# A seven-product down projection in four steps of the first token block, with the second block's residual rows parked in device memory

## The chip, the cores and the metric

The kernel runs on one core of one Trainium2 chip. The metric is the device time of one execution in microseconds (us), the median of a few executions. TensorE multiplies matrices, VectorE and ScalarE read its results from PSUM, GpSimd works on SBUF, and SyncE issues the DMAs. The profile calls them PE (PEld for its weight loads), DVE, ACT, POOL and SP. In a program each engine executes its own instructions strictly in the order in which they were written.

## What is computed

The input x is 2048 tokens by 640 features in float32. Two sublayers with a residual each:

```python
h  = x + irfft2(rfft2(layernorm(x)) * (w_r + 1j * w_i))     # spectral filter over tokens and features
z  = layernorm(h)
h2 = h + ((z @ w_gate) * (z @ w_up)) @ w_down               # bilinear GLU, 640 -> 1728 -> 640
```

The change touches the second sublayer alone, and what of the first one's output waits for it.

## The kernel before, in words

**Number format.** Every matrix operand of the GLU is held as two float32r parts, a high and a low one. A product of two operands is three matmuls: high by high, high by low, low by high. "Splitting" a tile means that ACT writes the high part and DVE or POOL the low part.

**Tiles and blocks.** The 2048 tokens are 16 tiles of 128 rows. The first sublayer ends with one addition per tile into the residual rows `X[t]` (`acc`, L505). Tiles 0 to 7 are token block 0 and lie in the SBUF buffer `XH[0]` (tag `xh0`); tiles 8 to 15 are block 1 and lie in `XH[1]` (tag `xh1`). Each is 128 by 8 x 641 float32. All through block 0 of the GLU the rows of block 1 lie idle in `xh1`: they are only read, for the mean and variance and at the end to be normalised.

**Steps.** For each block the 1728 hidden features are 14 chunks, taken in seven steps of two chunks: step `p` holds chunks 2p and 2p+1, and the order is 6, 0, 1, 2, 3, 4, 5 (L1009). Step 6 is computed plainly. In the others `strassen` (L929) makes gate and up of one chunk for the block's 1024 tokens, as two halves of 512, with 54 matmuls of 512 columns; its products go to three PSUM banks called `p11`, `acc_a` and `p53`. ACT copies `acc_a` to `p1` (L960), later to `u2` (L973) and `p53` to `m5` (L979); DVE adds `p11` into `p1` (L970). The hidden tiles that come out are kept split in numbered units of `ht` (`unit`, L723); unit 6 lies in the buffer `ex`.

**The down projection of a step runs inside the next step.** There are two forms.

- Plain (`down`, L747): for each of the 8 token tiles of the block 12 matmuls of 320 columns (10 for step 6), then one DVE addition into `X[t]` (L508). The 8 tiles are called between the products of the next step's first chunk (`some`, L933), and after each one entry of the list `fill` is executed (L937): block 0 uses that list for the 32 small operations that take mean and variance of block 1's rows (L132 to L161).
- Seven-product (`mixed_down`, L884): the 2 by 2 block product with seven block products in place of eight, 84 matmuls in place of 96, in 16 pieces that are woven one by one behind the matmul triples of the next step's first chunk (`tick`, L943). It takes other hidden operands (`mixed_first` and `mixed_second`, which form sums and differences on DVE), other weight operands (`load_mixed`, L849, sums on POOL), and room for them: `EX[0]`, 128 by 8 x 641, which holds half of the weight operands (`wo`) and unit 6, called `ex` in the profile. What DVE and ACT still owe of the hidden units when a woven chunk begins is the list `pending`; `flush(1)` executes one entry after each woven piece.

Before the change steps 0 to 4 of **block 1** are seven-product. `EX[0]` is then the buffer of block 0's rows, which are finished and written out (L1090). Block 0 has plain steps only, since both row buffers are in use.

**The passage from block 0 to block 1.** In chunk 11 of block 0 SP loads the plain weights of chunks 13 and 12 (`load_direct`, one DMA to `draw`, two to `raw`), ACT takes their high parts (`wdir`, L463, by side[1], right after the `p1` addition), and ACT normalises the eight tiles of block 1 (L525, by side[2]). Then eight plain downs of step 5 alternate with the transposes of the normalised tiles (L1045 to L1058), and 90 matmuls against `wdir` follow.

**Weights.** `load_raw` brings 640 KB of chunk weights to `stage` (called `raw`); `prep` turns them into split operands with ACT and POOL. All DMAs named here are issued by SP, in the order in which the program names them, and SP does not go past one whose wait is not over.

Of the kernel before, what the change touches and what calls it, by code (L numbers as in the profile page):

```python
# [46 lines left out]
def tile_spectral_glu(ctx: ExitStack, tc: tile.TileContext, x, wf, wgu, wlast, wdown, wdlast,  # L47
# [43 lines left out]
    XH = [keep.tile([P, 8 * (D + 1)], F32, tag=f"xh{h}", name=f"x{h}") for h in range(2)]  # L91
    XP = [XH[t // 8][:, t % 8 * (D + 1):(t % 8 + 1) * (D + 1)] for t in range(NT)]
    X = [xp[:, 0:D] for xp in XP]
    cct = keep.tile([P, P], F32, name="cct")
    ident = keep.tile([P, P], F32, name="ident")

# [408 lines left out]
    def acc(t, ps, total=None):  # L505
        xv = X[t].rearrange("p (a b) -> p a b", a=2)
        if total is None:
            tt(xv, ps[:, :, 0:320], xv, op=OP.add)  # L508
        else:
            nc.vector.scalar_tensor_tensor(xv, ps[:, :, 0:320], 1.0, xv, op0=OP.mult, op1=OP.add, accum_out=total)  # L510
# [152 lines left out]
    for t in range(NT):  # L663
        for k in tside[t]:
            turn_mm(k)
        if t + 2 < NT:
            unfold(t + 2, dside[t], tside[t])
        else:
            for k in tside[t]:
                turn_hi(k)  # L670
                turn_lo(k)
        if t + 3 < NT:
            id_mm(t + 3)
        for f in aside[t]:
            f()
        if t == NT - 3:
            ht = home("qm", [P, 8192], "ht", F32R)
            hts, t3 = cut(ht, 0, 3, 2, 2, 512), cut(ht, 6144, 2, 2, 512)
            banks("a", "pglu")
            gu(NC - 1, 0)  # L680
        is1_mm(t)
        acc(t, PY[t], total[:, t:t + 1] if t < 8 else None)
        if t == NT - 2:
            late = gate_parts(NC - 1, 0, 0)
    transp(6)
# [35 lines left out]
        return copies, sums, high, low  # L721

    def unit(u):  # L723
        v = ht[:, 1024 * u:1024 * u + 1024] if u < 6 else EX[0][:, (3840, 1920)[u - 6]:][:, 0:1024]
        return v[:, 0:512], v[:, 512:1024]

    def high_of(u, src):
        act(unit(u)[0], src, AF.Copy)  # L728
# [56 lines left out]
    def flush(n=8):  # L785
        for h in pending[:n]:
            h()
        del pending[:n]
# [140 lines left out]
    def strassen(c, blk, h, ahead, downs, side, fine=()):  # L929
# [3 lines left out]
        def some(n):  # L933
            for _ in range(n):
                if downs:
                    downs.pop(0)()
                    pop(1)  # L937

        def at(n):
            for f in side.get(n, ()):  # L940
                f()

# [22 lines left out]
        if ahead and not woven:  # L965
# [1 line left out]
            flush(2)  # L967
            ahead[1]()
            flush()
        tt(p1, p11, p1, op=OP.add)  # L970
        at(1)
        product(acc_a, ws, 0, t2, start=False)
        act(u2, acc_a, AF.Copy)  # L973
        flush()
        if ahead and woven:
            ahead[0]()
            ahead[1]()
# [35 lines left out]
    for n, (blk, p) in enumerate(steps):  # L1013
        if p == 6:
# [28 lines left out]
            else:  # L1043
                copies, sums, high, low = prep(0, blk)
                js = [4, 5, 6, 7, 0, 1, 2, 3]  # L1045
                for j in range(8):
                    transp(8 + j)
                    if j >= 1:
                        down(*prev, js[j - 1], True)
                    if j % 4 == 3:  # L1050
                        fifth(range(5 + j, 9 + j))
                    if j == 3:
                        copies()
                        sums()
                    if j == 5:
                        high()
                        low()
                down(*prev, js[7], True)  # L1058
                gu(NC - 1, 0)
                gate_parts(NC - 1, 0, s13)()  # L1060
# [24 lines left out]
                fs, cs = scale_shift(range(8, 16), None)  # L1085
                fill.extend(fs + cs)
            continue
        mixed = blk == 1 and p < 5
        if mixed and p == 0:
            EX[0] = home("xh0", [P, 8 * (D + 1)], "ex", F32R)  # L1090
        wdn = load_mixed(p) if mixed else load_d(p)
        downs, fine = [], []
        if prev[2] is None:
# [3 lines left out]
        if mixed:  # L1097
            units, hs = None, (mixed_first(), mixed_second())
        else:
            units = [(2 * k, 2 * k + 1) for k in (count % 3, (count + 1) % 3)] if blk == 0 else [(2, 7), (1, 0)]  # L1100
            hs = [plain_h(u[1], u[0]) for u in units]
        for ci in range(2):
            c = 2 * p + ci
            side = {}
            ahead = None
            if c == 0:
                side[0] = [*t34(1), lambda j=first_wd: issue(j)]
            if c < 11:
                ahead = prep(c + 1, blk)
                side[5] = [lambda c=c: load_raw(c + 2)] if c < 10 else []  # L1110
            if ci == 0 and mixed:
                side[2] = [wdn[0], wdn[1]]
                side[6] = [wdn[2]]
            elif ci == 0:
                side[3] = [lambda wdn=wdn: issue(wdn)]
            if c == 11 and blk == 0:
                pop(len(fill))
                dj = load_direct(1, [wk([P, D], "draw"), stage[:, 0:640], stage[:, 640:1280]])
                side[1] = [lambda: issue(dj[0]), lambda: issue(dj[1]), lambda: load_raw(0)]

                def low(ks):
                    for k in ks:
                        if k == 0:
                            TJ["z"] = home("qr", [P, 6, D], "zt")
                        normalise(8 + k, TJ["z"][:, k] if k < 6 else wk([P, D], "z"))

                side[2] = [lambda: low(range(8))]
            strassen(c, blk, hs[ci], ahead, downs if ci == 0 else [], side, fine if ci == 0 else ())
            count += 1
        prev = (blk, p, units)  # L1130
# [134 lines left out]
```

## Time and profile before

| | |
|---|---|
| median of 3 runs | 721.1 us (720.89 to 722.38) |
| the profiled execution | 720.87 us |
| its span, first to last instruction | 719.1 us |
| mean granted TensorE clock | 1.000 |
| PE busy | 694.4 us, 97% |
| DVE, ACT, POOL busy | 445.0, 294.0, 333.8 us |

The profile below is of that one execution. A row of the timeline gives the start in us from the span's start, the busy time, the engine, the line of the kernel, the operation, the tiles (out<-in) and, in brackets, how long the engine stood idle before it and what ended that. A row of the windows gives for one stretch its length, then for each engine the busy time and the number of instructions (counting those that reach into it), then the clock column, the DMA share and the GB/s. In the rows, the matmuls of `strassen` write `e` and have 512 columns, those of the down projection write `y` and have 320.

### The profile page before, as it was taken

Reading aid. Unit: us, or ns where it says so; the run is one execution under the profiler, and the core shown is the slowest. Engines: PE = TensorE matmul, PEld = TensorE weight load, DVE = VectorE, ACT = ScalarE, POOL = GpSimd, SP = SyncE. Lnnn points to the kernel's source line nnn. Section 1 sums busy time; section 2 is a strip of 40 time slices with the busy share of each in tenths; the row PEclk is TensorE's granted clock in tenths of the full one; section 3 lists DMA queues with packets and bytes.
Section 4 is the critical chain, followed back from the end, with each engine's and each line's share of the span. In section 5 each row is a group of like instructions: output and inputs, shape, how many; then the busy total and the mean of one; then the engine's idle time right before and its main releaser. Section 6 shows DMA issues by size and latency. Waiting matters only on the chain.

```text
span 719.1 us, 10059 instructions
## 1 busy us (share of the span) xinstructions
PE 694.4 (97%) x3832; PEld 611.6 (85%) x3832; DVE 445.0 (62%) x787; ACT 294.0 (41%) x554; POOL 333.8 (46%) x310
## 2 busy tenths in 40 slices
PE   7899998999999999999999998999999999999998
PEld 7788997977878898989898988789888888888887
DVE  7968887797965453636334436565666666565654
ACT  4756666355543223223323245352334243424320
POOL 3300114332154554546454543138696877767610
PEclk9999999999999999999999999999999999999999
DMA  9405765000221212110011222221110203030203
GB/s 337 170 1 165 229 212 188 1 1 0 74 75 37 73 37 74 37 55 25 36 71 36 93 74 80 90 88 38 63 47 24 88 0 111 1 106 4 74 0 147
DMA packets 20927, 55.04 MB, mean 77 GB/s; under 512 B 2320, under 2 KB 6928, under 8 KB 20880
## 3 DMA queue, kind: packets, MB, share of 16 engines
q1 hardware_dynamic: 20304, 52.70, 21.3%
q0 software_dynamic: 288, 1.48, 0.6%
q8 instruction: 30, 0.49, 0.3%
q10 hardware_dynamic: 288, 0.23, 0.1%
q14 instruction: 17, 0.14, 0.1%
HBM read 49.16 MB, written 5.24 MB: 76 GB/s over the span
## 4 chain that ended last, share of the span: by engine, by line
PE 78%; DVE 13%; issue 4%; ACT 3%; POOL 1%; DMA 1%; DVEq 0%; POOLq 0%; ACTq 0%
PE e L82 42%; PE y L82 24%; PE re L82 2%; PE im L82 2%; PE u L341 2%; PE eo L82 2%; DVE fold L191 1%; DVE x L906 1%; DVE fold L196 1%; PE im L391 1%; PE im L390 1%; PE ir L382 1%; ACT zt L525 1%; DVE x L510 1%; DVE bits L215 1%
## 5 line engine op out<-in xcount | busy, mean ns | idle before, releaser
L82 PE MATMUL e<-xt,wst 128*128 128x512 f32 x864 | 214.6, 391 | 1.2 <-DVE ht L656 1.1
L82 PEld LDWEIGHTS e<-xt,wst 128*128 128x128 f32 x864 | 159.1, 188 | 30.9 <-DVE ht L656 1.6
L82 PE MATMUL y<-wd,ht 128*128 128x320 f32 x1048 | 171.3, 310 | 4.3 <-DVE x L508 3.1
L82 PEld LDWEIGHTS y<-wd,ht 128*128 128x128 f32 x1048 | 160.8, 188 | 13.3 <-DVE x L508 3.6
L703 POOL TENSOR_TENSOR wst<-raw,wst 128x1024 fp32r<-128x1024 f32 x24 | 57.9, 2412 | 113.2 <-ACT wst L702 108.0
L508 DVE TENSOR_TENSOR x<-y,x 128x640 f32<-128x640 f32 x79 | 65.0, 823 | 71.7 <-PE y L82 71.5
L728 ACT ACTIVATE ht<-e 128x512 fp32r<-128x512 f32 x47 | 27.5, 596 | 126.5 <-DVE e L797 101.0
L719 POOL TENSOR_TENSOR wst<-raw,wst 128x896 fp32r<-128x896 f32 (+1 forms) x46 | 65.1, 1438 | 21.4 <-ACT wst L714 21.4
L82 PE MATMUL e<-t,wst 128*128 128x512 f32 x288 | 71.9, 390 | 0.0
L906 DVE TENSOR_TENSOR x<-y,x 128x640 f32<-128x640 f32 x60 | 49.3, 823 | 28.4 <-PE y L82 28.0
L82 PEld LDWEIGHTS e<-t,wst 128*128 128x128 f32 x288 | 53.3, 188 | 9.7
L464 POOL TENSOR_TENSOR wd<-draw,wd 128x640 fp32r<-128x640 f32 x18 | 28.8, 1624 | 66.8 <-ACT wd L463 66.8
L986 DVE TENSOR_TENSOR m<-e,m 128x512 f32<-128x512 f32 x24 | 16.5, 689 | 52.1 <-PE e L82 51.6
L732 DVE TENSOR_TENSOR ht<-e,ht 128x512 fp32r<-128x512 f32 x47 | 32.2, 685 | 19.1 <-ACT ht L728 18.8
L82 PE MATMUL e<-xt,wdir 128*128 128x512 f32 x180 | 41.9, 392 | 1.1 <-DVE q L494 1.1
L82 PEld LDWEIGHTS e<-xt,wdir 128*128 128x128 f32 x180 | 33.5, 188 | 8.3 <-ACT xt L547 1.3
L702 ACT ACTIVATE wst<-raw 128x1024 fp32r<-128x1024 f32 x24 | 25.4, 1056 | 35.2 <-DMA raw<-in_wgu_dram 35.2
L714 ACT ACTIVATE wst<-raw 128x896 fp32r<-128x896 f32 (+1 forms) x48 | 30.0, 676 | 19.4 <-POOL raw L708 18.7
L82 PE MATMUL e<-ht,wst 128*128 128x512 f32 x144 | 37.7, 391 | 0.0
L207 PE MATMUL im<-bits,fold 128*128 128x128 f32 x192 | 30.0, 292 | 6.6 <-DVE fold L196 2.3
L409 POOL CAST qr<-bits 1x128 fp32r<-1x128 f32 x16 | 4.5, 280 | 68.0 <-DVE qr L406 68.0
L207 PEld LDWEIGHTS im<-bits,fold 128*128 128x128 f32 x192 | 24.6, 193 | 11.2 <-DVE fold L196 5.6
(210 smaller groups left out, 1165.0 us busy)
## 6 DMA issues: line engine op xcount, KB each, us to landing
raw<-in_wgu_dram SPq DMA_DIRECT2D x24, 640.0 KB, 3.9
wts<-in_wf_dram SPq DMA_DIRECT2D x16, 644.0 KB, 4.1
draw<-in_wdown_dram SPq DMA_DIRECT2D x24, 320.0 KB, 4.5
x<-in_x_dram SPq DMA_DIRECT2D x16, 320.5 KB, 6.0
out_dram<-x SPq DMA_DIRECT2D x15, 320.0 KB, 2.2
bits<-in_mm_dram SPq DMA_DIRECT2D x32, 128.0 KB, 3.9
raw<-in_wgu_dram SPq DMA_DIRECT2D x4, 320.0 KB, 3.8
draw<-in_wdlast_dram SPq DMA_DIRECT2D x4, 320.0 KB, 2.9
```

Of the source, the lines that this page charges most:

```text
L82: nc.tensor.matmul(o, l, r, start=start, stop=stop, skip_group_check=True)
L207: nc.tensor.matmul(pm[:, k * P:(k + 1) * P], l, c, start=n == 0, stop=n == len(ls) - 1)
L464: los.append(lambda r=r, a=a, b=b: engine.tensor_tensor(w[:, 1, a:b], r, f32(w[:, 0, a:b]), op=OP.subtract))
L508: tt(xv, ps[:, :, 0:320], xv, op=OP.add)
L702: act(wa[:, 0], stage[:, 0:1024], AF.Copy)
L703: nc.gpsimd.tensor_tensor(wa[:, 1], stage[:, 0:1024], f32(wa[:, 0]), op=OP.subtract)
L714: act(ws[:, 0, o:o + b - a], stage[:, a:b], AF.Copy)
L719: ptt(ws[:, 1, o:o + b - a], stage[:, a:b], f32(ws[:, 0, o:o + b - a]), op=OP.subtract)
L728: act(unit(u)[0], src, AF.Copy)
L732: engine.tensor_tensor(lo, src, f32(hi), op=OP.subtract)
L906: tt(xv, PQ[q][:, :, 0:320], xv, op=OP.add)
L986: tt(m5, acc_a, m5, op=OP.add)
```

## The change

Steps 1 to 4 of block 0 take the seven-product form too. To make room, the residual rows of block 1 go to device memory while block 0 runs its GLU.

- **Spill.** After the first sublayer's last addition to each of tiles 8 to 15, SP writes the tile to a DRAM tile `spill` (8 DMAs of 320 KB).
- **Room.** In block 0, `EX[0]` is the buffer `xh1`, taken at step 1. By then the mean and variance of block 1's rows have to be done, so the list `fill` is emptied in step 0: two entries behind each plain down instead of one, and five at each of the fixed places (`at`) of chunk 1.
- **Bring back.** `bring_back`, called ahead of chunk 11 of block 0, takes `xh1` again and has SP load the 8 tiles. It stands in the program ahead of `load_direct`. Normalising is spread over three places of chunk 11: four tiles at side[3], two at side[6], two at side[5].
- **The `p1` addition** stands behind the second product and the `flush` where the chunk is woven, in both blocks.
- **Units.** Step 5 keeps its hidden tiles in units 4, 2, 1, 0 in both blocks; the former unit 7 in `EX[0]` is gone.
- **Passage.** Among the eight last downs of block 0 the transposes of the fifth slices (`fifth`) come ahead of the down of the same turn, and the `high` and `low` splitting of chunk 0's weights comes after the loop.

```diff
@@ -91,6 +91,8 @@
     XH = [keep.tile([P, 8 * (D + 1)], F32, tag=f"xh{h}", name=f"x{h}") for h in range(2)]
     XP = [XH[t // 8][:, t % 8 * (D + 1):(t % 8 + 1) * (D + 1)] for t in range(NT)]
     X = [xp[:, 0:D] for xp in XP]
+    kept = ctx.enter_context(tc.tile_pool(name="kept", bufs=1, space=bass.MemoryType.DRAM))
+    spill = [kept.tile([P, D], F32, tag=f"sp{i}", name=f"sp{i}") for i in range(8)]
     cct = keep.tile([P, P], F32, name="cct")
     ident = keep.tile([P, P], F32, name="ident")
 
@@ -680,6 +682,8 @@
             gu(NC - 1, 0)
         is1_mm(t)
         acc(t, PY[t], total[:, t:t + 1] if t < 8 else None)
+        if t >= 8:
+            nc.sync.dma_start(spill[t - 8], X[t])
         if t == NT - 2:
             late = gate_parts(NC - 1, 0, 0)
     transp(6)
@@ -721,8 +725,15 @@
         return copies, sums, high, low
 
     def unit(u):
-        v = ht[:, 1024 * u:1024 * u + 1024] if u < 6 else EX[0][:, (3840, 1920)[u - 6]:][:, 0:1024]
+        v = ht[:, 1024 * u:1024 * u + 1024] if u < 6 else EX[0][:, 3840:4864]
         return v[:, 0:512], v[:, 512:1024]
+
+    def bring_back():
+        XH[1] = home("xh1", [P, 8 * (D + 1)], "xb")
+        for t in range(8, NT):
+            o = (t - 8) * (D + 1)
+            X[t] = XH[1][:, o:o + D]
+            nc.sync.dma_start(X[t], spill[t - 8])
 
     def high_of(u, src):
         act(unit(u)[0], src, AF.Copy)
@@ -934,9 +945,11 @@
             for _ in range(n):
                 if downs:
                     downs.pop(0)()
-                    pop(1)
+                    pop(2)
 
         def at(n):
+            if c == 1 and blk == 0:
+                pop(5)
             for f in side.get(n, ()):
                 f()
 
@@ -967,11 +980,14 @@
             flush(2)
             ahead[1]()
             flush()
-        tt(p1, p11, p1, op=OP.add)
+        if not woven:
+            tt(p1, p11, p1, op=OP.add)
         at(1)
         product(acc_a, ws, 0, t2, start=False)
         act(u2, acc_a, AF.Copy)
         flush()
+        if woven:
+            tt(p1, p11, p1, op=OP.add)
         if ahead and woven:
             ahead[0]()
             ahead[1]()
@@ -1045,16 +1061,15 @@
                 js = [4, 5, 6, 7, 0, 1, 2, 3]
                 for j in range(8):
                     transp(8 + j)
+                    if j % 4 == 3:
+                        fifth(range(5 + j, 9 + j))
                     if j >= 1:
                         down(*prev, js[j - 1], True)
-                    if j % 4 == 3:
-                        fifth(range(5 + j, 9 + j))
                     if j == 3:
                         copies()
                         sums()
-                    if j == 5:
-                        high()
-                        low()
+                high()
+                low()
                 down(*prev, js[7], True)
                 gu(NC - 1, 0)
                 gate_parts(NC - 1, 0, s13)()
@@ -1085,9 +1100,10 @@
                 fs, cs = scale_shift(range(8, 16), None)
                 fill.extend(fs + cs)
             continue
-        mixed = blk == 1 and p < 5
-        if mixed and p == 0:
-            EX[0] = home("xh0", [P, 8 * (D + 1)], "ex", F32R)
+        mixed = p < 5 and (blk == 1 or p > 0)
+        if p == 1 - blk:
+            pop(len(fill))
+            EX[0] = home(f"xh{1 - blk}", [P, 8 * (D + 1)], "ex", F32R)
         wdn = load_mixed(p) if mixed else load_d(p)
         downs, fine = [], []
         if prev[2] is None:
@@ -1097,7 +1113,7 @@
         if mixed:
             units, hs = None, (mixed_first(), mixed_second())
         else:
-            units = [(2 * k, 2 * k + 1) for k in (count % 3, (count + 1) % 3)] if blk == 0 else [(2, 7), (1, 0)]
+            units = [(2 * k, 2 * k + 1) for k in (count % 3, (count + 1) % 3)] if p == 0 else [(4, 2), (1, 0)]
             hs = [plain_h(u[1], u[0]) for u in units]
         for ci in range(2):
             c = 2 * p + ci
@@ -1114,7 +1130,7 @@
             elif ci == 0:
                 side[3] = [lambda wdn=wdn: issue(wdn)]
             if c == 11 and blk == 0:
-                pop(len(fill))
+                bring_back()
                 dj = load_direct(1, [wk([P, D], "draw"), stage[:, 0:640], stage[:, 640:1280]])
                 side[1] = [lambda: issue(dj[0]), lambda: issue(dj[1]), lambda: load_raw(0)]
 
@@ -1124,7 +1140,9 @@
                             TJ["z"] = home("qr", [P, 6, D], "zt")
                         normalise(8 + k, TJ["z"][:, k] if k < 6 else wk([P, D], "z"))
 
-                side[2] = [lambda: low(range(8))]
+                side[3] = [lambda: low(range(4))]
+                side[6] = [lambda: low((4, 5))]
+                side[5] = [lambda: low((6, 7))]
             strassen(c, blk, hs[ci], ahead, downs if ci == 0 else [], side, fine if ci == 0 else ())
             count += 1
         prev = (blk, p, units)
```

**SP, at the end of block 0's step 5 (chunks 10 and 11).** `in_wdown` is the down weight of step 5, `in_wlast` and the two rows of 128x640 behind it are the loads that ACT's `wdir` takes; the bracket names the semaphores waited for (DMAHW: an earlier DMA's landing; PE: a matmul). Before:

```order
L462 DMA draw_3405<-in_wdown_dram 128x640 [waits DMAHW3_49]
L462 DMA draw_3406<-in_wdown_dram 128x640 [waits DMAHW4_49]
L462 DMA draw_3608<-in_wlast_dram 128x640 [waits DVE_49]
L462 DMA raw_1814<-in_wgu_dram 128x640 [waits DMAHW6_49,Pool_49]
L462 DMA raw_1814<-in_wgu_dram 128x640
L691 DMA raw_1814<-in_wgu_dram 128x1280 [waits DMAHW3_49,DMAHW2_49,Pool_49]
```

And now (`sp0` to `sp7` are the spilled tiles, `xb` the buffer `xh1` as it is taken again):

```order
L464 DMA draw_3480<-in_wdown_dram 128x640 [waits DMAHW0_49,DVE_49]
L736 DMA xb_3679<-sp0_70 128x640 [waits DVE_49,PE_49]
L736 DMA xb_3679<-sp1_71 128x640
L736 DMA xb_3679<-sp2_72 128x640 [waits DMAHW3_49]
L736 DMA xb_3679<-sp3_73 128x640 [waits DMAHW4_49]
L736 DMA xb_3679<-sp4_74 128x640
L736 DMA xb_3679<-sp5_75 128x640 [waits DMAHW6_49]
L736 DMA xb_3679<-sp6_76 128x640 [waits DMAHW7_49]
L736 DMA xb_3679<-sp7_77 128x640 [waits DMAHW0_49]
L464 DMA draw_3688<-in_wlast_dram 128x640 [waits DMAHW1_49]
L464 DMA raw_1832<-in_wgu_dram 128x640 [waits DMAHW2_49,Pool_49]
L464 DMA raw_1832<-in_wgu_dram 128x640 [waits DMAHW3_49]
```

Eight loads stand ahead of the three, and the first of the eight waits for the last matmul that reads `ex`, which is the last matmul of chunk 10.

**ACT, in chunk 11 of block 0.** `p1`, `u2` and `m5` are the copies out of PSUM, `zt` and `z` the normalised tiles, `ht` the hidden tiles, `xt` and `bt` the transposed ones. Before:

```order
L960 ACTIVATE p1_3622<-e_3614 128x512
L463 ACTIVATE wdir_3609<-draw_3608 128x640
L463 ACTIVATE wdir_3609<-raw_1814 128x640 x2
L973 ACTIVATE u2_3623<-e_3614 128x512
L979 ACTIVATE m5_3624<-e_3615 128x512
L525 ACTIVATE zt_3660<-x1_67,b_1923,r_1922 128x640 x6
L525 ACTIVATE z_3667<-x1_67,b_1923,r_1922 128x640
L525 ACTIVATE z_3669<-x1_67,b_1923,r_1922 128x640
L728 ACTIVATE ht_1714<-e_3615 128x512
L728 ACTIVATE ht_1714<-e_3614 128x512
```

And now:

```order
L973 ACTIVATE p1_3702<-e_3694 128x512
L465 ACTIVATE wdir_3689<-draw_3688 128x640
L465 ACTIVATE wdir_3689<-raw_1832 128x640 x2
L987 ACTIVATE u2_3703<-e_3694 128x512
L995 ACTIVATE m5_3704<-e_3695 128x512
L739 ACTIVATE ht_1729<-e_3695 128x512
L527 ACTIVATE zt_3759<-xb_3679,b_1941,r_1940 128x640 x6
L739 ACTIVATE ht_1729<-e_3694 128x512
L527 ACTIVATE z_3779<-xb_3679,b_1941,r_1940 128x640
L527 ACTIVATE z_3781<-xb_3679,b_1941,r_1940 128x640
```

The three `wdir` rows keep their place between `p1` and `u2`; the normalising moved behind the first hidden tile.

**DVE, at the start of the first woven chunk of block 1 (chunk 2).** `y` is the PSUM of the down projection, `rawh` a held difference, `ex` unit 6, whose low part is the row that ends in `ex<-e,ex`. Before:

```order
L906 TENSOR_TENSOR x1_67<-y_4681,x1_67 128x2x320
L843 TENSOR_TENSOR e_4568<-e_4568,rawh_4636 128x512
L970 TENSOR_TENSOR p1_4674<-e_4665,p1_4674 128x512
L906 TENSOR_TENSOR x1_67<-y_4690,x1_67 128x2x320
L732 TENSOR_TENSOR ex_4062<-e_4568,ex_4062 128x512
L906 TENSOR_TENSOR x1_67<-y_4681,x1_67 128x2x320
```

And now:

```order
L917 TENSOR_TENSOR xb_3679<-y_4459,xb_3679 128x2x320
L854 TENSOR_TENSOR e_4346<-e_4346,rawh_4414 128x512
L917 TENSOR_TENSOR xb_3679<-y_4468,xb_3679 128x2x320
L743 TENSOR_TENSOR ex_4142<-e_4346,ex_4142 128x512
L917 TENSOR_TENSOR xb_3679<-y_4459,xb_3679 128x2x320
L990 TENSOR_TENSOR p1_4452<-e_4443,p1_4452 128x512
```

The `p1` row went from ahead of unit 6's low part to behind it; the addition of the second tile stayed ahead of it.

## The prediction

> **What bounds the kernel now.** I read the page first, for the engine that sets the end.
>
> ```profile
> PE 694.4 (97%) x3832; PEld 611.6 (85%) x3832; DVE 445.0 (62%) x787; ACT 294.0 (41%) x554; POOL 333.8 (46%) x310
> PE   7899998999999999999999998999999999999998
> PE 78%; DVE 13%; issue 4%; ACT 3%; POOL 1%; DMA 1%; DVEq 0%; POOLq 0%; ACTq 0%
> ```
>
> PE is busy for 97% of the span, in nearly every slice, and holds 78% of the chain that ended last. So a matmul that goes is worth its full time, and a wait that PE did not have costs its full time. Next the windows: a plain pair of chunks in block 0 (6 and 7 in step 3, with the downs of step 2), the same pair in block 1, where the downs are woven, and block 1's woven chunk 10, whose own step is plain. Each window is cut where PE starts its second set of products.
>
> ```profile
> 357.66:384.06 26.40, 26.40 (x151) 24.20 (x150) 11.18 (x15) 7.17 (x11) 12.32 (x11) 1.00 0.21 75
> 384.06:396.30 12.24, 12.24 (x55) 10.14 (x54) 4.77 (x7) 4.03 (x7) 7.66 (x7) 1.00 0.00 0
> 591.97:615.74 23.77, 23.33 (x128) 20.74 (x127) 16.23 (x24) 8.24 (x13) 17.80 (x16) 1.00 0.24 84
> 615.74:629.76 14.02, 14.02 (x67) 11.88 (x66) 7.63 (x13) 5.94 (x11) 10.51 (x9) 1.00 0.00 1
> 667.56:692.10 24.54, 23.62 (x128) 20.68 (x127) 16.41 (x24) 7.05 (x11) 12.01 (x10) 1.00 0.16 54
> ```
>
> A chunk without downs has 54 matmuls of 512 columns in 12.24 us, 0.2267 us each. The plain chunk has 96 of 320 columns more and takes 14.16 us more, 0.1475 us each, without any stall (PE is busy for all 26.40). The woven pair has 84: 72 in the first window, 12 in the second. The second is 12.24 + 12 x 0.1475 = 14.01, as measured. The first should be 12.24 + 10.62 = 22.86 and is 23.77: **a woven chunk loses 0.91 us**. A plain pair is 38.64 us, a woven one 37.79: of the 1.77 us that 12 matmuls are worth, half comes through. Chunk 10 loses another 0.77 (24.54).
>
> **Part 1, the matmuls.** Steps 1 to 4 of block 0 lose 12 matmuls each: 48 x 0.1475 = **-7.08 us**.
>
> **Part 2, the loss in the woven chunks.** Most of it is one wait:
>
> ```profile
> 555.15 0.69 DVE L843 TENSOR_TENSOR e<-e,rawh 128x512 f32<-128x512 f32 x1
> 555.75 0.68 DVE L970 TENSOR_TENSOR p<-e,p 128x512 f32<-128x512 f32 x1
> 556.35 0.82 DVE L906 TENSOR_TENSOR x<-y,x 128x640 f32<-128x640 f32 x1
> 557.08 0.68 DVE L732 TENSOR_TENSOR ex<-e,ex 128x512 fp32r<-128x512 f32 x1
> 557.82 0.42 PE L82 MATMUL y<-ex 128*128 128x320 f32 x1 [0.44 <-DVE ex L732]
> PE y L82 <- DVE ex L732: 2.2, 5, 0.4
> ```
>
> PE waits for the low part of unit 6, in all five woven chunks. The DVE runs four operations end to end ahead of it, and the change takes the `p1` addition (L970) out from among them. The addition of the second tile (L906) stays ahead, and cannot start before its six matmuls end:
>
> ```profile
> 554.90 1.04 PE L82 MATMUL y<-wd,ht 128*128 128x320 f32 x6
> ```
>
> They end at 555.94. So L906 starts at about 555.97 in place of 556.35, and the low part comes 0.38 us earlier. I take -0.38 per woven chunk: 0.53 is left of 0.91. Bounds: 0 (a slower POOL or ACT takes its place) and -0.91 (all of it goes). The `p1` addition (0.68) then stands ahead of the next L906 of the second tile, for which the DVE now waits 0.74; it is covered, and without that cover would cost its 0.68.
>
> ```profile
> 559.84 0.83 DVE L906 TENSOR_TENSOR x<-y,x 128x640 f32<-128x640 f32 x1 [0.74 <-PE y L82]
> ```
>
> Block 0 gets four woven chunks: 4 x 0.53, and in chunk 10 the further 0.77, whose wait is after the chunk's last products and not touched: **+2.89 us**. Block 1 has five: 5 x -0.38 = **-1.90 us**. That block 0 weaves as well as block 1 rests on POOL and DVE having the same work there: in the window of 591.97 they are busy for 17.80 and 16.23 of 23.77 us, in block 0's plain one for 12.32 and 11.18 of 26.40, so there is room. Step 1 of block 0 forms the new hidden operands beside plain downs, as step 0 of block 1 does now:
>
> ```profile
> 478.38:502.43 24.05, 24.05 (x135) 21.86 (x134) 12.17 (x16) 8.11 (x14) 20.84 (x17) 1.00 0.09 28
> ```
>
> 54 x 0.2267 + 80 x 0.1475 = 24.04: no stall, so nothing is charged.
>
> **Part 3, the bring-back.** This is what decides. In chunk 11 now:
>
> ```profile
> 417.32 0.80 SPq L462 DMA_DIRECT2D raw<-in_wgu_dram  x2
> 419.28 3.59 PE L82 MATMUL e<-xt,wst 128*128 128x512 f32 x15
> 421.41 0.73 ACT L463 ACTIVATE wdir<-draw 128x640 fp32r<-128x640 f32 x1
> 422.04 1.36 ACT L463 ACTIVATE wdir<-raw 128x640 fp32r<-128x640 f32 x2
> 424.26 0.60 ACT L973 ACTIVATE u<-e 128x512 f32<-128x512 f32 x1 [0.86 <-PE e L82]
> 426.10 1.52 PE L82 MATMUL e<-ht,wst 128*128 128x512 f32 x6
> ```
>
> PE begins chunk 11 at 419.28 (call it T). The three weight loads are issued before T, ACT's `wdir` is done by 423.4, `u2` (L973) waits for PE and not the other way round, and PE goes on into `acc_a`, which `u2` reads, at T + 6.82. After the change the three loads stand on SP behind eight loads of 320 KB, and the first of these waits for the last matmul of chunk 10, so it is issued at about T + 0.2. How fast eleven such loads come in, the start of the program shows (16 loads of 320.5 KB in a row), and the first landing a load into an empty queue:
>
> ```profile
> 4.80:18.80 14.00, 10.51 (x76) 9.46 (x74) 13.51 (x49) 7.77 (x23) 6.77 (x10) 1.00 1.05 401
> draw<-in_wdlast_dram SPq DMA_DIRECT2D x4, 320.0 KB, 2.9
> ```
>
> At 401 GB/s with all 16 DMA engines taken, 320 KB are 0.82 us. The first lands at T + 3.1, the eleventh at T + 3.1 + 10 x 0.82 = T + 11.3. ACT, which comes to `wdir` at T + 2.8, stands still for these loads with `u2` queued behind: the last `wdir` ends at T + 12.1, `u2` at T + 12.7, and PE goes on there instead of at T + 6.82: **+5.9 us**, between +5.0 (if a first landing takes 2.2 us as the output writes do) and +6.8.
>
> **Part 4, the clock after that wait.** The longest waits of PE in the list of waits are these, the nearest rows to a PE that comes from idleness are the program's first matmuls:
>
> ```profile
> PE y L82 <- DVE x L508: 3.1, 2, 1.6
> ```
>
> ```profile
> 1.06:6.44 5.38, 5.38 (x25) 5.38 (x26) 0.00 (x0) 1.00 0.82 266
> 6.45:9.00 2.55, 2.55 (x25) 2.55 (x24) 0.00 (x0) 1.00 1.04 403
> ```
>
> No wait is over 1.6 us, so no row shows what 5.9 us do. At the start the same 25 instructions take 5.38 us and then 2.55 us (the clock column says 1.00 for both; the durations tell). If the wait brings this state back, PE loses half of 5.38, **+2.7 us**, on the path, since PE works without a pause from T + 12.7. Bounds 0 and 2.8; I take 2.7, the row that it is nearest to. [...]
>
> **Part 5, the rest of the passage.**
>
> ```profile
> 431.53:454.55 23.02, 19.39 (x137) 18.45 (x136) 15.87 (x27) 12.38 (x22) 8.42 (x7) 1.00 0.22 86
> 426.86 4.98 ACT L525 ACTIVATE zt<-x,b,r 128x640 f32<-128x640 f32 x6
> 436.27 0.61 ACT L551 ACTIVATE bt<-e 128x512 f32<-128x512 f32 x1
> 436.75 0.62 ACT L547 ACTIVATE xt<-e 128x512 fp32r<-128x512 f32 x1
> 443.86 0.60 PE L537 MATMUL e<-ident,zt 128*128 128x128 f32 x4
> 444.21 2.01 PE L82 MATMUL y<-wd,ht 128*128 128x320 f32 x12
> 452.69 2.03 PE L82 MATMUL y<-wd,ht 128*128 128x320 f32 x12 [1.64 <-DVE x L508]
> ```
>
> From chunk 11's end to the first `wdir` matmul are 23.02 us, of which 8 downs (96 x 0.1475 = 14.2) and 10 groups of four transposes (0.35 from the first to what follows, 443.86 to 444.21) are 17.7: 5.3 us of waits. After the change normalising begins only behind the first hidden tile, so the first transposes wait 1.1 us for it and the second and fourth 0.8 together. ACT needs 8 x 0.83 for the tiles and 0.48 for each of the 8 copies behind them, so the fifth slices wait about 2.4 us and the third down 1.4. The late waits (as 1.64 at 452.69) go, since `high` and `low` leave the loop. 5.7 us in all: **+0.4 us**, between -3 (ACT keeps up) and +2.
>
> **Part 6, small.** The spill puts the first raw weights behind the last tile's addition:
>
> ```profile
> 181.59 0.33 SPq L691 DMA_DIRECT2D raw<-in_wgu_dram  x1
> 182.85 0.80 DVE L508 TENSOR_TENSOR x<-y,x 128x640 f32<-128x640 f32 x1
> 187.51 1.05 ACT L702 ACTIVATE wst<-raw 128x1024 fp32r<-128x1024 f32 x1
> ```
>
> The issue moves from 181.59 to about 184.1, the landing from 185.5 to about 188, 0.5 us past the copy at 187.51. The 32 operations of `fill`, some 9 us of DVE, crowd into step 0; a plain pair leaves the DVE idle for over half its time. **+0.4 us** for both, 0 to 1.5.
>
> **Sum**, against the profiled execution's 720.87 (0.2 below the median of 721.1): -7.08 + 2.89 - 1.90 + 5.9 + 2.7 + 0.4 + 0.4 = +3.3, so **724.2 us**.
>
> **Rivals.**
>
> 1. *The wait comes, the clock stays.* Without the 2.7: 721.5 us, no change that can be told. For it: the bounds of part 4; against: the slow first 5.38 us. It decides whether the matmuls behind the wait last longer than before it. Chance 0.20.
> 2. *The weaving loses nothing more.* If the `p1` addition was what kept the whole 0.91 us, all nine woven chunks gain another 0.53: 724.2 - 4.8 = 719.4 us, faster. For it: the wait for `ex` is the only one PE has in chunks 2 to 9 of block 1; against: L906 stays ahead of the low part. It decides from 0.3 us left per chunk on, with the clock slow. Chance 0.18.
> 3. *The change doesn't do what it says.* Block 0's weaving, with new waits on POOL or DVE, costs as much as the 48 matmuls bring: the 4.2 us of parts 1 and 2 are missing, 728.4 us. Chance 0.07.
>
> **How the numbers follow.** My forecast has 0.55; its own range is 722.5 to 726.5 by the bounds of parts 3 to 6. The range that should hold 8 times in 10 takes in rival 1 and reaches into rivals 2 and 3: 718.0 to 727.0. A measurement of this kernel tells about 0.2%, 1.4 us, from no change. Faster by more, below 719.7: rival 2 and a tail of rival 1, 0.20. Within: the rest of rival 1 and the low end of the forecast, 0.20. Slower: 0.60.
>
> **What would show it.** Parts 1 and 2: block 0's pairs of steps 2 to 4 at about 37.4 us, with 84 matmuls of 320 columns. Part 3: `wdir` on ACT idle for some 7 us before it, ended by a DMA, and PE waiting 5.9 us for ACT's `u2`. Part 4: matmuls of 0.45 us apart behind that wait. Part 5: PE starts on `wdir` 28.9 us after the end of the wait (426.10 to 454.55, 28.45, before), and what part 4 adds. I am wrong if the weight loads land by T + 4.9, which would take 11 x 320 KB in 4.7 us, 770 GB/s, or if SP need not wait for chunk 10's last matmul.

## The result, and the profile after

The changed kernel takes **727.09 us** in the median (726.67 to 727.62), the kernel before beside it 721.1: a ratio of 1.008 (95% interval 1.0062 to 1.0097), 6.0 us slower. The profiled execution took 726.67 us, its span is 724.9 (before 720.87 and 719.1), its mean granted clock 0.990 (1.000).

The same three places of the page of after: busy times, the slices of PE, the chain.

```profile
PE 694.0 (96%) x3784; PEld 607.1 (84%) x3784; DVE 477.9 (66%) x839; ACT 305.5 (42%) x574; POOL 367.0 (51%) x342
...
PE   7999998999999999999999967999999999999998
...
PE 77%; DVE 12%; issue 4%; DMA 4%; ACT 2%; POOL 0%; SPq 0%; DVEq 0%; POOLq 0%; ACTq 0%
```

PE has 48 matmuls less, but is busy for only 0.4 us less, since some run longer. DMA takes 4% of the chain in place of 1%. Two slices are no longer full, 6 and 7 tenths (each slice is 18.1 us long): chunk 11 of block 0 and the passage.

Next the windows of after for a pair of chunks in block 0 (4 and 5 in step 2, with the downs of step 1, plain before and woven now), the same for block 1, and block 1's chunk 10, cut as before; columns as in the prediction.

```profile
282.63:306.06 23.43, 23.34 (x129) 20.67 (x127) 16.32 (x24) 8.26 (x13) 17.58 (x16) 1.00 0.25 86
306.06:320.10 14.04, 14.04 (x68) 11.89 (x67) 7.64 (x13) 5.93 (x11) 10.76 (x10) 1.00 0.00 1
561.45:584.87 23.42, 23.33 (x128) 20.74 (x127) 16.34 (x24) 8.23 (x13) 17.50 (x16) 1.00 0.25 85
584.87:598.89 14.02, 14.02 (x67) 11.88 (x66) 7.63 (x13) 5.94 (x11) 10.88 (x10) 1.00 0.01 1
673.69:697.90 24.21, 23.57 (x129) 20.59 (x127) 16.52 (x24) 7.05 (x11) 12.00 (x10) 1.00 0.16 55
```

The woven pair of block 0 takes 37.47 us (38.64 plain, as every plain pair of block 0 from chunk 2 on); the same window of block 1 fell from 23.74 to 23.42. That part works. Now chunk 11, whose first products begin at T = 415.81 (before: 419.28), on SP, PE and ACT:

```profile
416.00 3.80 SPq L736 DMA_DIRECT2D xb<-sp  x8
419.85 0.70 SPq L464 DMA_DIRECT2D draw<-in_wlast_dram  x1
420.65 1.08 SPq L464 DMA_DIRECT2D raw<-in_wgu_dram  x2
```

```profile
415.81 3.62 PE L82 MATMUL e<-xt,wst 128*128 128x512 f32 x15
419.27 2.88 PE L82 MATMUL e<-t,wst 128*128 128x512 f32 x12
421.99 0.84 PE L82 MATMUL e<-xt,wst 128*128 128x512 f32 x3
429.44 2.93 PE L82 MATMUL e<-ht,wst 128*128 128x512 f32 x6 [6.61 <-ACT u L987]
432.17 5.18 PE L82 MATMUL e<-xt,wst 128*128 128x512 f32 x18
```

```profile
418.05 0.59 ACT L973 ACTIVATE p<-e 128x512 f32<-128x512 f32 x1
426.58 0.74 ACT L465 ACTIVATE wdir<-draw 128x640 fp32r<-128x640 f32 x1 [7.94 <-DMA draw<-in_wlast_dram]
428.81 0.58 ACT L987 ACTIVATE u<-e 128x512 f32<-128x512 f32 x1
```

Read from the bottom: `u2` comes right behind `wdir`, `wdir` waited 7.94 us for a DMA, PE waited 6.61 us for `u2`. Six matmuls of 512 columns take 2.93 us behind the wait, and took 1.52 before. PE goes on at T + 13.63, where it was T + 6.82.

Last, stretches of after around that wait and in the passage. I cut them at the changes of the clock, which the trace records there at 427.27, 434.10, 447.75 and 451.16.

```profile
423.86:427.26 3.40, 0.00 (x0) 0.00 (x0) 0.00 (x0) 0.68 (x1) 0.00 (x0) 1.00 0.98 388
427.28:434.09 6.81, 4.65 (x11) 3.68 (x12) 0.69 (x1) 2.49 (x5) 4.57 (x3) 0.50 0.14 44
434.11:437.35 3.24, 3.24 (x14) 2.32 (x13) 1.40 (x2) 0.54 (x2) 0.00 (x0) 1.00 0.27 111
444.34:447.74 3.40, 0.66 (x4) 0.42 (x4) 2.10 (x4) 3.40 (x9) 0.00 (x0) 1.00 0.00 0
447.76:451.15 3.39, 3.33 (x12) 3.33 (x13) 2.52 (x5) 1.93 (x4) 1.33 (x1) 0.50 0.50 193
437.36:462.14 24.78, 20.75 (x136) 19.87 (x137) 16.71 (x28) 16.36 (x27) 7.34 (x6) 0.93 0.21 80
```

The clock column has two half-rate stretches here. One follows the long wait. The other lies in the passage, behind 3.40 us in which PE did only four transposes (0.66 us). No single wait there is over 1.94 us (a row of this list gives the total, the number of waits and the longest):

```profile
PE e L570 <- DVE xt L557: 1.9, 1, 1.9
PE y L82 <- DVE x L510: 1.0, 1, 1.0
```

The trace of after has a third half-rate stretch, from 17.67 to 21.08 us in the first sublayer, and that of before has none there. It costs nothing that can be told: PE starts chunk 0's products at 201.22 us (201.09 before).

**Where the 5.8 us of the span came from**: PE reaches chunk 11 3.47 us earlier; the wait costs 6.81 (13.63 - 6.82); the rest of chunk 11 takes 7.91 in place of 5.43 (429.44 to 437.35), +2.48; the passage takes 24.80 in place of 23.02, +1.78; the next 23.8 us, up to the second products of block 1's chunk 0, are the same; the rest of block 1 takes 238.93 in place of 240.72, -1.79. Together +5.8.

### The profile page after: what moved, and what is told of

It is laid out like the page before. It is cut to its first block, busy times and chain, and to the rows that moved or that the text cites. A ratio compares the mean times of both kernels' runs of the same rounds, so it can differ in the third digit from the quotient of the medians.

```text
span 724.9 us, 10120 instructions
## 1 busy us (share of the span) xinstructions
PE 694.0 (96%) x3784; PEld 607.1 (84%) x3784; DVE 477.9 (66%) x839; ACT 305.5 (42%) x574; POOL 367.0 (51%) x342
## 4 chain that ended last, share of the span: by engine, by line
PE 77%; DVE 12%; issue 4%; DMA 4%; ACT 2%; POOL 0%; SPq 0%; DVEq 0%; POOLq 0%; ACTq 0%
PE e L82 41%; PE y L82 24%; PE re L82 2%; PE im L82 2%; PE u L343 2%; PE eo L82 2%; DMA raw<-in_wgu_dram 2%; DVE fold L193 1%; DVE fold L198 1%; PE im L393 1%; PE im L392 1%; PE ir L384 1%; DVE ex L743 1%; DMA x<-in_x_dram 1%; DVE xb L917 1%
## 5 line engine op out<-in xcount | busy, mean ns | idle before, releaser
L82 PE MATMUL e<-xt,wst 128*128 128x512 f32 x864 | 220.4, 393 | 1.3 <-DVE ht L658 1.2
L82 PE MATMUL y<-wd,ht 128*128 128x320 f32 x880 | 152.4, 312 | 2.4 <-DVE x L510 1.0
L82 PEld LDWEIGHTS y<-wd,ht 128*128 128x128 f32 x880 | 139.9, 190 | 14.9 <-DVE x L510 1.3
L82 PE MATMUL e<-t,wst 128*128 128x512 f32 x288 | 74.1, 391 | 0.0
L917 DVE TENSOR_TENSOR xb<-y,xb 128x640 f32<-128x640 f32 x60 | 49.4, 824 | 26.0 <-PE y L82 24.2
L917 DVE TENSOR_TENSOR x<-y,x 128x640 f32<-128x640 f32 x48 | 39.5, 824 | 20.9 <-PE y L82 20.0
L82 PE MATMUL e<-ht,wst 128*128 128x512 f32 x144 | 39.8, 403 | 6.6 <-ACT u L987 6.6
L82 PE MATMUL y<-ex,ht 128*128 128x320 f32 x216 | 43.4, 309 | 0.0
L466 POOL TENSOR_TENSOR wd<-draw,wd 128x640 fp32r<-128x640 f32 x10 | 16.3, 1653 | 49.6 <-ACT wd L465 49.6
L510 DVE TENSOR_TENSOR x<-y,x 128x640 f32<-128x640 f32 x32 | 26.2, 820 | 21.7 <-PE y L82 21.7
L82 PEld LDWEIGHTS y<-ex,ht 128*128 128x128 f32 x216 | 36.2, 188 | 3.2
```

What stands on the lines that cost most here:

```text
L82: nc.tensor.matmul(o, l, r, start=start, stop=stop, skip_group_check=True)
L466: los.append(lambda r=r, a=a, b=b: engine.tensor_tensor(w[:, 1, a:b], r, f32(w[:, 0, a:b]), op=OP.subtract))
L917: tt(xv, PQ[q][:, :, 0:320], xv, op=OP.add)
```

## The experiments

My theory: the eight bring-back loads, which stand on SP ahead of the three weight loads, make the wait, and PE's idleness makes the slow clock. The rivals: the wait comes with the eleven loads in whatever order, and the slowness is that of loads or other engines. All times are medians; the kernel before took 720.8 to 721.1 us beside them.

### weights_first: 718.4 us

```diff
-                bring_back()
                 dj = load_direct(1, ...)
+                bring_back()
```

> The changed kernel with one edit: SP issues the three weight loads of block 1's wdir ahead of the eight bring-back loads, not behind them. Theory (the order on the SP queue makes the wait): wdir on ACT is ready by about T + 4 as in the kernel before, PE's wait of 6.6 us for u2 goes, and with it the slow clock behind it (2.5 us): 727.1 - 6.8 - 2.5 = 717.8 us; if the second slow stretch in the passage (1.6 us, at 447.75) hangs on the wait too, 716.2 us. Rival (the eleven loads hold up chunk 11 whatever their order, now through the normalising on ACT, which needs the rows brought back): PE still waits some 5 us in chunk 11 or right behind it, and the time stays above 722 us.

Measured 718.4 us (717.62 to 718.7), ratio to before 0.9964 (0.9950 to 0.9977). The wait is gone and chunk 11 runs through:

```profile
421.58 0.84 PE L82 MATMUL e<-xt,wst 128*128 128x512 f32 x3
422.26 1.52 PE L82 MATMUL e<-ht,wst 128*128 128x512 f32 x6
423.62 4.24 PE L82 MATMUL e<-xt,wst 128*128 128x512 f32 x18
```

**The order on the one queue made the wait.** One edit of order, with the same eleven loads, takes 8.7 us. The slow stretch of the passage did not go with the wait; it is twice as long here. The first window is the whole passage, the second the stretch ahead of the half rate, the third the half rate:

```profile
427.87:453.82 25.95, 21.91 (x136) 21.02 (x137) 16.83 (x28) 16.36 (x27) 7.35 (x6) 0.87 0.20 77
433.89:437.29 3.40, 1.47 (x11) 0.89 (x9) 1.23 (x3) 3.40 (x8) 0.00 (x0) 1.00 0.00 0
437.32:444.12 6.80, 5.78 (x22) 5.74 (x23) 5.00 (x9) 3.49 (x6) 3.62 (x3) 0.50 0.32 124
```

So the passage has a cause of its own.

### four_ahead: 723.34 us

```diff
-                bring_back()
+                bring_back(range(8, 12))
                 dj = load_direct(1, ...)
+                bring_back(range(12, NT))
```

> The changed kernel with four bring-back loads ahead of the three weight loads and four behind them. Theory of the queue: the last weight load lands four loads of 0.83 us earlier, PE waits 3.3 us in place of 6.6: -3.3 us, 723.8 us. Theory of the clock (only a wait above some length between 1.6 and 6.6 us brings the half rate): if 3.3 us is below that length, the 2.5 us behind the wait go too, 721.3 us, and 719.7 us without the second slow stretch. Rival (the wait is set by when the queue starts, not by the number of loads ahead): 727.1 us, unchanged.

Measured 723.34 us (722.23 to 724.92). The queue's price holds in the main: four loads less ahead shorten the wait from 6.61 to 3.71 us (3.3 expected). One of the two outcomes that I gave for the clock, that it stays full after a shorter wait, does not come: it is still halved, for 3.4 us. The row of that wait, then the stretches around it:

```profile
428.16 1.77 PE L82 MATMUL e<-ht,wst 128*128 128x512 f32 x6 [3.71 <-ACT u L988]
```

```profile
426.16:429.55 3.39, 1.39 (x6) 1.17 (x7) 0.00 (x0) 2.35 (x4) 3.39 (x3) 1.00 0.82 323
429.57:432.96 3.39, 3.39 (x10) 2.64 (x9) 0.69 (x1) 0.00 (x0) 1.06 (x1) 0.50 0.35 128
```

The stretch ahead of this half rate held 1.39 us of PE work. It was not idle, only less than half busy. (This trace is the slowest of the five executions, 724.92 us. It comes to chunk 11's second products at 420.88, 1.61 us later than the change at 419.27, and why is not shown.)

### warm_wait: 725.0 us

```diff
+        if c == 11 and blk == 0:
+            spare = pair("y")
+            for _ in range(26):
+                mmx(spare[:, 0], wa[:, 0, 384:512], b11[0][0], True, True)
         product(acc_a, ws, 640, ...)
```

> The changed kernel with 26 matmuls of 128x512 into a spare bank, which nothing reads, put into PE's wait of 6.6 us (26 x 0.2267 = 5.9 us of it). Theory (PE's idleness brings the half rate): the matmuls behind the wait run at 0.2267 us, 2.5 us less, 724.6 us, and 723.0 us if the second slow stretch goes too. Rival (the slowness behind the wait is that of the loads or of the other engines, not of PE's idleness): 727.1 us, with matmuls 0.45 us apart as before.

Measured 725.0 us (724.4 to 726.73), in the median 2.1 less than the change; 26 more matmuls make it faster. The wait ends 10.41 us after the chunk's second products begin (10.17 in the change), and what follows runs at full rate: 5.75 us to the end of chunk 11 in place of 7.91.

```profile
422.23 6.05 PE L82 MATMUL y<-xt,wst 128*128 128x512 f32 x26
429.24 1.66 PE L82 MATMUL e<-ht,wst 128*128 128x512 f32 x6 [0.95 <-ACT u L987]
```

```profile
429.24:434.99 5.75, 5.75 (x24) 4.42 (x24) 2.09 (x3) 0.96 (x3) 2.56 (x2) 1.00 0.31 112
```

The eleven loads and the instructions of ACT, DVE and POOL are those of the change, since the edit adds matmuls alone; the clock column behind the wait says 1.00 here and 0.50 there (up to 434.09). **PE's idleness made the first slow stretch**, not the loads. The second stretch stayed, as in weights_first.

### p1_old and before_p1: 730.98 and 719.18 us

p1_old puts the `p1` addition of the changed kernel back; before_p1 makes only that move in the kernel before, as shown:

```diff
-        tt(p1, p11, p1, op=OP.add)
+        if not woven:
+            tt(p1, p11, p1, op=OP.add)
         ...
         flush()
+        if woven:
+            tt(p1, p11, p1, op=OP.add)
```

> The changed kernel with the p1 addition of the woven chunks back where it stood, ahead of unit 6's low part. Theory (the addition held up the low part): each of the nine woven chunks loses 0.36 to 0.38 us again, 9 x 0.37 = +3.3, 730.4 us, with PE's wait for ex back at 0.4 us. Rival (the shorter woven chunks come from another part of the change): 727.1 us, unchanged.

> The kernel before with one edit: the p1 addition of block 1's woven chunks moved behind unit 6's low part, as in the change. Theory (it held up the low part): five woven chunks shorter by 0.36 us each, 721.1 - 1.8 = 719.3 us. Rival (the low part waits for something else in the kernel before, or the later addition holds up the next one): 721.1 us or more.

p1_old took 730.98 us (729.12 to 732.65), before_p1 719.18 (719.01 to 720.74; ratio 0.9975, 0.9966 to 0.9984). A woven window of p1_old, its list of waits, and a woven window of before_p1:

```profile
319.91:343.69 23.78, 23.33 (x129) 20.67 (x127) 16.22 (x24) 8.25 (x13) 17.75 (x16) 1.00 0.24 83
```

```profile
PE y L82 <- DVE ex L743: 4.0, 9, 0.4
```

```profile
553.95:577.37 23.42, 23.33 (x129) 20.74 (x128) 16.33 (x24) 8.26 (x13) 17.53 (x16) 1.00 0.25 85
```

Nine windows lose 0.34 to 0.38 us each when the addition comes back, with PE's wait for `ex` nine times; five gain 0.33 to 0.38 when it alone moves (9 x 0.35 = 3.2; the profiled executions of p1_old and the change are 2.5 us apart, the medians 3.9, and what else is in that I did not follow). The addition held up unit 6's low part, as the prediction said.

### early_norm, fifth_behind and early_norm_fifth: 713.54, 718.99 and 713.74 us

These ask what makes the gap in the passage. All start from weights_first. early_norm:

```diff
-                side[3] = [lambda: low(range(4))]
-                side[6] = [lambda: low((4, 5))]
-                side[5] = [lambda: low((6, 7))]
+                side[2] = [lambda: low(range(8))]
```

fifth_behind puts the fifth slices behind the down that follows, as the kernel before has them; early_norm_fifth has both edits:

```diff
-                    if j % 4 == 3:
-                        fifth(range(5 + j, 9 + j))
                     if j >= 1:
                         down(*prev, js[j - 1], True)
+                    if j % 4 == 3:
+                        fifth(range(5 + j, 9 + j))
```

> As weights_first, and all eight tiles of block 1 normalised in chunk 11 at the place where the kernel before does it (behind the copy m5), not in three pieces behind the two hidden tiles. In weights_first ACT stands idle for 4.2 us there (423.1 to 427.3) while the rows land (418.5 to 425.8), PE waits 1.9 and 1.0 us around the fifth slices, and the second slow stretch costs some 2.9 us. Theory (the late normalising makes the gap, the sparse stretch makes the slow clock): both waits shrink and the clock stays full, 718.4 - 2.9 = 715.5 us or up to 1.5 us less. Rival 1 (the order in the passage makes the gap, the fifth slices ahead of the third down): 718.4 us, unchanged. Rival 2 (normalising now waits for the rows with the copies of the hidden tile queued behind it): PE waits again in chunk 11 and the time is above 719.5 us.

> As weights_first, and the fifth slices again behind the down that follows, as in the kernel before; normalising stays late. Theory (a stretch in which PE has little to do is enough for the slow clock, without one long wait): the third down (12 matmuls, 1.77 us) runs inside the gap, PE is busy for over half of each 3.4 us there, no slow stretch, 718.4 - 2.9 = 715.5 us, and up to 1.8 us less if the wait itself shrinks by the down. Rival (the slow stretch comes whatever stands there, from the loads or as a repeat after a slow stretch): 718.4 us with the half rate still in the passage.

> early_norm and fifth_behind together. If each removes the same gap, the sum is no better than the better one: about 715 us. If ACT is what the passage waits for (late normalising) and the order only hides it, early normalising alone is enough and this gives the same as early_norm within 0.5 us.

Measured: early_norm **713.54 us** (713.01 to 714.91), ratio to before 0.9898 (0.9886 to 0.9911), the fastest kernel of the study. early_norm_fifth is the same, 713.74 (713.49 to 713.87). fifth_behind, of which I expected 715.5, is no gain: 718.99 (717.33 to 721.13). Its third down waits too, on PE:

```profile
434.12 0.66 PE L539 MATMUL e<-ident,zt 128*128 128x128 f32 x4
438.40 3.57 PE L82 MATMUL y<-wd,ht 128*128 128x320 f32 x12 [3.62 <-DVE x L510]
```

and DVE of the same kernel shows for what:

```profile
435.96 0.69 DVE L557 TENSOR_TENSOR xt<-e,xt 128x512 fp32r<-128x512 f32 x1 [1.90 <-ACT bt L553]
436.92 0.69 DVE L557 TENSOR_TENSOR xt<-e,xt 128x512 fp32r<-128x512 f32 x1 [0.27 <-ACT bt L553]
437.53 0.81 DVE L510 TENSOR_TENSOR x<-y,x 128x640 f32<-128x640 f32 x1
```

The first down's addition (L510), which frees the PSUM pair that the third down needs, stands on DVE behind the low parts of transposed slices (L557), and these wait for ACT's copies. So the order on PE does not matter while ACT is late. Why ACT is late, two rows of weights_first and two of early_norm tell (the last is the third `bt` copy, which weights_first makes at 437.18):

```profile
427.33 0.60 ACT L739 ACTIVATE ht<-e 128x512 fp32r<-128x512 f32 x1 [4.21 <-DVE e L808]
427.82 4.97 ACT L527 ACTIVATE zt<-xb,b,r 128x640 f32<-128x640 f32 x6
```

```profile
423.56 4.98 ACT L527 ACTIVATE zt<-xb,b,r 128x640 f32<-128x640 f32 x6
434.89 0.65 ACT L553 ACTIVATE bt<-e 128x512 f32<-128x512 f32 x1
```

Normalising starts 4.26 us earlier, in ACT's idle time ahead of the hidden tile. ACT waits there for none of the rows brought back: the first six tiles run end to end in 4.98 us, and the last two follow in 1.72. The passage of early_norm then takes 20.50 us, against 25.95 in weights_first and 23.02 before, at full clock:

```profile
428.42:448.92 20.50, 18.95 (x137) 18.27 (x135) 16.55 (x28) 12.20 (x22) 7.39 (x6) 1.00 0.25 98
```

### hold4, hold6, hold7 and hold9: 715.02, 718.28, 718.61 and 720.72 us

By now half-rate stretches had followed stretches that were partly busy. These four have one wait of 1.23 to 4.38 us each. Each is early_norm with more copies of `u2`, so that PE waits in an otherwise full chunk; 7 copies in hold6, as shown, and 5, 8 and 10 in hold4, hold7 and hold9:

```diff
-        act(u2, acc_a, AF.Copy)
+        for _ in range(7 if c == 3 and blk == 1 else 1):
+            act(u2, acc_a, AF.Copy)
```

> early_norm, and in chunk 3 of block 1 (a plain chunk) ACT makes the copy u2 seven times over in place of once, 6 x 0.48 us more. PE, which has 2.0 us of products between, waits 0.7 + 6 x 0.48 - 2.04 = 1.5 us there. Theory (the clock is granted for stretches of 3.41 us, and halves after one in which PE was busy for less than about half): 1.5 us leave every such stretch busy for 0.55 or more, no slow clock: 713.5 + 1.5 = 715.0 us. Rival (only a wait that covers a whole stretch of 3.41 us halves the clock): the same, 715.0 us.

> As hold6, with eight copies: PE waits 2.0 us. Theory of half a stretch: where the wait lies with over 1.7 us in one stretch (6 times in 10, by chance of where the stretches fall), the next 3.41 us run at half rate and cost 1.7 us more: 715.5 us in some runs, 717.2 in others. Rival (a whole stretch of idleness is needed): 715.5 us in all runs, no half rate in the trace.

> As hold6, with ten copies: PE waits 3.0 us. Theory of half a stretch: nearly always (9 in 10) a half rate of 3.41 us behind it: 713.5 + 3.0 + 1.7 = 718.2 us. Rival (a whole stretch of idleness is needed): 716.5 us, no half rate in the trace.

> As hold6, with five copies. hold6, hold7 and hold9 showed waits of 2.5, 3.1 and 4.4 us, 0.62 per copy, so this one is some 1.3 us. Theory of half a stretch: 1.3 us leave a stretch of 3.41 us busy for 0.62 at least, so there is no half rate behind the wait and the kernel costs the wait alone: 713.5 + 1.3 = 714.8 us. Rival (any wait of PE that is over a microsecond brings the half rate): 716.5 us, with a half rate behind the wait in the trace.

A copy took 0.63 us, not 0.48, so the waits came out longer than planned, and the times that I had given for hold6, hold7 and hold9 (715.0, 715.5 to 717.2, and 718.2) were passed by 1.4 to 3.3 us:

| | PE's wait | median, range | half rate behind it (profiled) |
|---|---|---|---|
| hold4 | 1.23 us | 715.02, 714.78 to 716.47 | none |
| hold6 | 2.49 us | 718.28, 715.93 to 719.61 | 3.41 us |
| hold7 | 3.12 us | 718.61, 717.93 to 721.15 | 3.41 us |
| hold9 | 4.38 us | 720.72, 719.45 to 722.22 | 3.78 us or more |

For hold9 the rows of PE behind the wait tell it, eight matmuls that take 3.78 us (in hold4 the first six took 1.66):

```profile
541.79 2.93 PE L82 MATMUL e<-ht,wst 128*128 128x512 f32 x6 [4.38 <-ACT u L988]
544.52 1.05 PE L82 MATMUL e<-xt,wst 128*128 128x512 f32 x2
```

The two stretches around the wait, in hold4, hold6 and hold7:

```profile
536.97:540.36 3.39, 2.16 (x10) 1.47 (x9) 0.00 (x0) 2.17 (x4) 3.08 (x5) 1.00 0.00 0
540.39:543.78 3.39, 3.39 (x17) 2.81 (x16) 1.94 (x3) 0.00 (x0) 1.44 (x2) 1.00 0.01 2
```

```profile
537.28:540.69 3.41, 0.92 (x5) 0.57 (x4) 0.00 (x0) 3.06 (x6) 3.17 (x5) 1.00 0.00 0
540.70:544.10 3.40, 3.40 (x10) 2.62 (x9) 0.69 (x1) 0.00 (x0) 1.00 (x1) 0.50 0.00 0
```

```profile
538.07:541.45 3.38, 0.93 (x4) 0.80 (x5) 0.00 (x0) 2.79 (x5) 3.22 (x4) 1.00 0.00 0
541.48:544.87 3.39, 3.39 (x10) 2.59 (x9) 0.69 (x1) 0.00 (x0) 0.19 (x1) 0.50 0.01 2
```

Behind the waits of 2.49 and 3.12 us, each shorter than the 3.41 us of half rate that follow it, the clock column says 0.50. Behind that of 1.23 us it says 1.00, and the kernel costs about the wait alone (713.54 + 1.23 = 714.8, 715.02 measured). **The rival that asks for a whole idle stretch falls**: the stretches ahead of the half rate held 0.92 and 0.93 us of PE work. The prices about add up, with half of each half-rate stretch as an estimate of its cost: hold7 is 713.54 + 3.12 + 1.7 = 718.4 (718.61 measured), hold6 717.7 (718.28), hold9 at least 713.54 + 4.38 + 1.9 = 719.8 (720.72). One execution of hold6, not the traced one, took 715.93 us at a mean clock of 0.999, and 713.54 and the bare wait are 716.0: so it seems to have paid for the wait alone, and why is not shown.

## Why the prediction was right in sign, and what was mis-sized

The forecast was +3.3 us over the profiled execution; +5.8 came. The median of 727.09 us lies at the upper end of the range, 0.1 us past it. The main mechanism, the loads ahead of the weights and the clock behind the wait, was as predicted, and the rivals fell: the clock did slow down (rival 1), the weaving kept over 0.5 us of loss per chunk (rival 2 needed less than 0.3), and block 0's weaving brought its share (rival 3). What the forecast missed is the size of part 3 and, in part 5, a second slow stretch that it left out. By the steps:

- **Parts 1 and 2.** 48 matmuls are gone. A woven chunk loses 0.57 us in block 0 and 0.52 to 0.56 in block 1 (0.53 predicted, from 0.91). Block 0 loses 4 x 0.57 + 0.81 in chunk 10 + 4 x 0.03 in the second windows, 3.2 in all (2.89 predicted); block 1 gains 1.79 (1.90). p1_old and before_p1 show the cause of the gain. The loss that is left is hardly a wait: PE is busy for 23.34 of the 23.43 us, so its matmuls take 0.48 us longer than the 22.86 of the sum, as they did before (23.33), and why stays open. (The prediction's plain pair at 357.66 is chunks 8 and 9, not 6 and 7; the plain pairs are alike, so the sum stands.)
- **Part 3, mis-sized: +5.9 predicted, +6.81 measured**, the upper bound. (The lower bound of +5.0 should be +5.2 by its own figures: 0.7 us off a first landing of 2.9.) The mechanism is shown by weights_first, and the dose by four_ahead. The first load landed at T + 3.06 (3.1 predicted), but the eleven took 9.28 us from the first landing to the last in place of 10 x 0.82 = 8.2. Eight of the ten steps were 0.77 to 0.86 us; from the second to the third load it took 1.67 and to the fourth 1.04. SP issued it 0.48 us behind the second in the change, so the issuing did not hold it up. Why stays open.
- **Part 4: +2.7 predicted, +2.48 measured**, with the matmuls 0.427 us apart (0.45 predicted) in place of 0.227. The price came from the program's start, where the clock column says 1.00; the clock records in the trace of before begin only at 6.44 us, so that column is no reading there, and the doubled durations were the right sign. warm_wait shows that PE's idleness is the cause.
- **Part 5, the other mis-sized term: +0.4 predicted, +1.78 measured.** The change in the waits was right. Before, PE is idle for 23.02 - 19.39 = 3.63 us there, after for 24.78 - 20.75 = 4.03: +0.40. That is in part luck: the prediction's own levels, 5.3 and 5.7 us, were both some 1.7 too high, since its 17.7 us of work are 19.39 in the window. The other 1.36 us are PE's own time, 20.75 in place of 19.39, for the same matmuls at half rate. The step that failed is that I asked what the waits cost and not what they do to the clock, since each was under 2 us; they stand together with only four transposes between. early_norm shows that the late normalising, which the change brings with the late rows, made them.
- **Part 6: +0.4 predicted, +0.45 measured**: 0.09 up to chunk 0's second products, 0.05 in chunk 0 and 0.31 in chunk 1 (12.55 in place of 12.24). So the crowded `fill` list made nearly all of it. The spill moved ACT's first weight copy from 187.51 to 188.87, more than the 0.5 us predicted, and PE's 0.09 is small beside that.

On the clock the traces say more than the prediction had: the half rate lasted 6.83 us behind the long wait and 3.41 us in the passage, and gaps of 2.49 and 3.12 us (hold6, hold7) were followed by it, and so was a stretch of 3.40 us with 1.47 us of PE work (weights_first).

## What to carry to other kernels

When loads are added, ask what already stands behind them on the same queue and who waits for that: here 2.6 MB that nobody needs for some 7 us stood ahead of 0.96 MB that ACT needed at once, and changing that order, with one more on ACT, turned 0.8% slower into 1.0% faster. Price a wait of the bound engine twice, its length and what the clock takes behind it (6.81 and 2.48 us here). And look for short waits that stand close together: no wait in the passage of after was over 1.94 us, and yet half rate came behind 3.40 us in which PE was busy for 0.66.

## What the runs showed of the hardware that was not expected

**Half rate came behind stretches in which PE did some work, not behind idle ones alone.** In the stretch of about 3.4 us just ahead of the half rate PE was busy for 0.00 and 0.66 us in after, 0.92 in hold6, 0.93 in hold7, 1.39 and 1.29 in four_ahead and 1.47 in weights_first. Two stretches of 3.39 us that were followed by a clock of 1.00 held 1.75 us (before, in its passage) and 2.16 us (hold4). What lies between 1.47 and 1.75 us, and whether other stretches would do the same, these rows don't tell, and the busy times go by PE's modelled ends. Half rate also lasted on with PE at work: in weights_first for 6.80 us, of which PE was busy for 5.78. The rows of before and the second pair of four_ahead:

```profile
450.19:453.58 3.39, 1.75 (x13) 1.50 (x12) 3.10 (x6) 1.28 (x3) 2.27 (x2) 1.00 0.04 15
453.61:457.00 3.39, 3.39 (x19) 2.98 (x18) 2.47 (x4) 0.00 (x0) 0.00 (x0) 1.00 0.48 186
```

```profile
443.22:446.61 3.39, 1.29 (x8) 1.06 (x9) 2.81 (x5) 3.39 (x8) 0.00 (x0) 1.00 0.00 0
446.63:450.02 3.39, 3.39 (x16) 3.35 (x15) 2.64 (x4) 1.32 (x3) 2.04 (x1) 0.50 0.50 193
```

**The time and the mean clock of one kernel differ from run to run**: hold6 took 715.93 to 719.61 us at mean clocks of 0.999 to 0.990. Of the 23 executions of the kernel before beside hold6, hold7 and hold9, 18 took 720.6 to 721.2 us and five 722.3 to 722.6. The difference is about 1.6 us, near the 1.7 that I estimate for a half-rate stretch of 3.41 us. That a sparse passage makes a kernel less steady is a guess by this, and not shown: the slower executions have no traces.
